# Transformer block: LN1 statistics of every second token tile on ScalarE, two min-adds of each q group on GpSimd, GpSimd's weight sums paced, two weight loads moved

## The chip, the cores and the metric

One core of one Trainium2 chip. The metric is device microseconds of one launch. The kernel before takes 759.02 us (median of 3 runs, 758.44 to 759.21). Engine names in the profile: PE is TensorE's matmuls, PEld its weight loads, DVE is VectorE, ACT is ScalarE, POOL is GpSimd ("Pool" below), SP is SyncE, which issues the DMAs. A bank is one of the buffers in PSUM in which TensorE adds up its products; a copy, sum or phi must have read it before TensorE can use it again.

## The reference

```python
# S=2048 tokens, D=1024, H=32 heads of 32, F=3584, inputs and weights bf16
phi = lambda t: where(t > 0, t + 1, exp(t)) + 1e-6
q, k, v = layernorm(x) @ wqkv          # split in three, by head
kv  = einsum("bhsd,bhse->bhde", phi(k), v)
z   = phi(k).sum over tokens
o   = (phi(q) @ kv) / (phi(q) . z + 1e-6)
h   = x + o @ wo
g   = layernorm(h)
h2  = h + (relu(g @ W_gate) * (g @ W_up)) @ W_down
```

(`gate * (gate > 0)` in the reference is the relu; the rest of its text sets up random inputs.)

## The kernel before

The kernel works in stages: the start and plain pieces for the first four token tiles; then, alternating, groups for k and v; q groups, in two halves of the tokens; the output projection; and the FFN in two passes of gate/up and down. The three projections use a scheme that forms a 2x2 block product from seven products (`P1` to `P7`) instead of eight, with sums of weights (`w_sums`, on Pool for q and v) and of tokens (`x_sums`, on VectorE) formed ahead.

One group, the same code for k, v and q. Seven products on TensorE; ScalarE copies (`ident_act`) fork one PSUM bank into another; what follows from a finished bank (`e11` to `e22`) is handed on in `pend` into the next group:

```python
def sgroup(pool, tok_major, X, SX, W, TW, e11, e12, e21, e22, name, hooks=()):
    # ... prod(): KH matmuls into one bank;  hook(i): pend[i] of the last group, then hooks[i]
    a = alloc_bank(pool); f = alloc_bank(pool); b = alloc_bank(pool)
    prod(a, X(0, 0), W(0, 0), True, "P1")
    ident_act(bank(b), bank(a), ..., name + "fk1")
    hook(1)
    prod(f, SX(2), TW(2), True, "P7")
    ident_act(s7, bank(f), ..., name + "s7")
    hook(2)
    c = alloc_bank(pool)
    prod(b, SX(1), TW(1), False, "P6")
    ident_act(bank(c), bank(b), ..., name + "fk2")
    hook(3)
    prod(a, X(1, 0), W(1, 0), False, "P2")
    # ... e11 on bank a
    hook(4)
    prod(c, SX(0), TW(0), False, "P5")
    ident_act(sc, bank(c), ..., name + "sc")
    # ... first step of e22
    hook(5)
    prod(b, X(1, 1), TW(3), False, "P4")
    # ... first step of e21
    hook(6)
    prod(c, SX(3), W(1, 1), False, "P3")
    pend[1] = list(e12(bank(c), B_bank[c]))
    pend[2] = list(s22[1:])
    pend[3] = list(s21[1:])
    hook(7)
```

phi is three operations: exp on ScalarE, then on VectorE a min-add, `min(e, 1) + 1e-6`, and `max(x + C1, that)`. The last one frees the PSUM bank or the SBUF buffer that it reads:

```python
def fin():
    PL.add("dve", lambda e: e.tensor_scalar(out=Et[:, k, :], in0=Et[:, k, :], scalar1=1.0,
                                            scalar2=1e-6, op0=ALU.min, op1=ALU.add), ...)   # "_e2"
    PL.add("dve", lambda e: e.scalar_tensor_tensor(out=dst_ap, in0=src, scalar=C1, in1=Et[:, k, :],
                                                   op0=ALU.add, op1=ALU.max), ...)          # "_phi"
```

LN1's statistics are on VectorE, the last step (variance to the power -0.5) on Pool, and each call of `ln1_stats` also issues a burst of Pool's weight sums behind it:

```python
def ln1_stats(st):
    i = st % NX1
    ln1_k[st] = ln_stats(x1[:, i, :], B_x1[i], "ln1_%d" % st)
    run(pool_q, {5: 8, 6: 5, 7: 4, 8: 5, 9: 5, 10: 5}.get(st, 7) if st >= 5 else 0)
```

In the output stage SyncE asks for transposes of `o`, for residual tiles, and, at some steps, for FFN weights; the down-projection weights (`load_wraw`) follow at its end:

```python
for t in range(NE, NST + LAG + 1):
    # ... a4 (output projection of tile t - LAG), a2 (num, division, transposes of tile t)
    if t in (5, 7, 9, 11, 18, 19):
        load_w_next()                 # 512 KB of gate or up weights
for q in range(NWR):
    load_wraw(q)
```

## Time and profile before

| TensorE's landmarks, from the trace | stage, us |
|---|---|
| start, to the first k piece | 7.79 |
| plain pieces and k group 2 | 32.14 + 20.55 |
| k and v groups 3 to 7 ("k/v stage" below) | 65.98 |
| q groups, first half / second half | 32.01 / 22.55 |
| output projection | 64.43 |
| FFN pass 0: gate/up, down | 169.43, 84.39 |
| FFN pass 1: gate/up, down and end | 169.21, 88.27 |

A stage ends at the first matmul of the next one, so a wait is counted in the stage that it delays. (The q halves and the output stage overlap by a few products at their landmarks. In this trace the record of the first matmul of FFN pass 0's down stage is missing: 0.22 us of the 169.43 belong to the 84.39.)

The head of the page, with the busy time of each engine in us (share of the span) and its number of instructions:

```profile
span 756.8 us, 10080 instructions
PE 737.7 (97%) x3547; PEld 337.2 (45%) x3603; DVE 545.6 (72%) x1083; ACT 291.2 (38%) x500; POOL 82.3 (11%) x148
```

TensorE is busy 737.7 of 756.8 us. (56 matmul records are missing from this trace, 3547 of 3603, so the true idle time is rather smaller than 19.1 us.) The list of TensorE's waits says on whom it waited (total us, times, longest):

```profile
PE ps L602 <- ACT ps L607: 3.9, 7, 1.2
PE ps L602 <- DMA RE<-RE: 2.3, 3, 1.2
PE ps L602 <- ACT RX L607: 1.9, 2, 0.9
```

`L607` is `ident_act`, so lines one and three are fork copies and copies to SBUF; the second is the transposes of `o` in the output stage. A q group of the second half in the timeline (start, length, engine, line, operation; in brackets the idle time before it and what ended it):

```profile
162.05 0.29 DVE L644 TENSOR_SCALAR RX<-RX 128x512 bf16<-128x512 bf16 x1
162.37 0.64 ACT L640 ACTIVATE RX<-RX 128x512 bf16<-128x512 f32 x1
162.38 0.69 DVE L647 SCALAR_TENSOR_TENSOR RAB<-ps,RX 128x512 bf16<-128x512 f32 x1
162.44 1.03 PE L602 MATMUL ps<-RAB,RO 128*128 128x512 bf16 x4
163.05 0.29 DVE L644 TENSOR_SCALAR RX<-RX 128x512 bf16<-128x512 bf16 x1
...
163.38 0.69 DVE L647 SCALAR_TENSOR_TENSOR RAB<-RX 128x512 bf16<-128x512 f32 x1
...
163.74 1.04 PE L602 MATMUL ps<-RWG,RH 128*128 128x512 f16 x4 [0.27 <-ACT ps L607]
```

exp (`L640`), min-add (`L644`, 0.29 us) and phi (`L647`, 0.69 us) follow each other, and TensorE loses 0.27 us in this stretch. The start (ScalarE's copies of the transposes, then the first k piece), and two of TensorE's longest waits in the k/v stage:

```profile
7.05 1.09 ACT L691 ACTIVATE RAB<-ps 128x512 bf16<-128x512 bf16 x2 [4.42 <-PE ps L688]
7.79 1.89 PE L602 MATMUL ps<-RAB 128*128 128x512 bf16 x8
...
80.58 1.04 PE L602 MATMUL ps<-RAB,RH 128*128 128x512 bf16 x4 [0.94 <-ACT RX L607]
...
84.58 1.04 PE L602 MATMUL ps<-RC,RWG 128*128 128x512 f16 x4 [1.23 <-ACT ps L607]
```

Two lines of the groups of work on Pool, which will matter later (busy us, mean ns of one):

```profile
L739 POOL TENSOR_TENSOR RW<-RAB 128x256 f16<-128x256 bf16 x16 | 13.4, 836 | 1.0
...
L1102 POOL TENSOR_TENSOR RO<-RWG 128x512 f16<-128x512 bf16 x4 | 4.6, 1153 | 0.0
```

### The profile page before, as it was taken

The page shows a single profiled execution, that of the slowest core. Times are in us where ns is not written, and L with a number is a line of the kernel's source. Part 1 is how long each engine was busy: PE and PEld are TensorE (multiplying, and loading weights), DVE is VectorE, ACT ScalarE, POOL GpSimd, SP SyncE. Part 2 cuts the span into 40 slices and gives each one's busy share as a digit, 9 for nine tenths or more (in the row PEclk, how much of TensorE's full clock was granted, in tenths as well). Part 3 has the DMA queues.
Part 4 walks back from the last instruction along what each step waited for, and adds up shares of the span by engine and source line. Part 5 has one row for each costly group of instructions (what it writes and reads, how often), then busy time and mean ns, then how long its engine had stood idle before and what let it go on. Part 6 is the DMA issues. An engine that isn't in the chain of part 4 may idle for free.

```text
span 756.8 us, 10080 instructions
## 1 busy us (share of the span) xinstructions
PE 737.7 (97%) x3547; PEld 337.2 (45%) x3603; DVE 545.6 (72%) x1083; ACT 291.2 (38%) x500; POOL 82.3 (11%) x148
## 2 busy tenths in 40 slices
PE   8999889999999999999999999999999999999998
PEld 3444334344544444444444444444444444444443
DVE  7978885889766798878877584847768686663343
ACT  4344545665850545454454100025454544520000
POOL 2746730000360000000000000000000000000000
PEclk9999999999999999999999999999999999999999
DMA  9753112402799786665445799743232231026664
GB/s 301 199 84 85 29 28 100 166 15 55 180 238 240 234 274 200 186 174 169 139 139 178 227 289 284 229 143 111 61 108 85 83 111 56 1 77 185 207 191 134
DMA packets 160225, 113.38 MB, mean 150 GB/s; under 512 B 51504, under 2 KB 141360, under 8 KB 160176
## 3 DMA queue, kind: packets, MB, share of 16 engines
q1 hardware_dynamic: 160176, 112.75, 52.3%
q8 instruction: 28, 0.46, 0.2%
q14 instruction: 21, 0.17, 0.1%
HBM read 85.46 MB, written 15.73 MB: 134 GB/s over the span
## 4 chain that ended last, share of the span: by engine, by line
PE 84%; DVE 8%; ACT 2%; issue 2%; SPq 1%; DMA 1%; POOL 0%; DVEq 0%; ACTq 0%; POOLq 0%
PE ps L602 84%; ACT ps L607 1%; DVE RX L644 1%; DVE RAB L647 1%; SPq L512 1%; DVE RE L647 1%; DVE RE L989 1%; DVE RWG L764 1%; ACT RX L640 1%; DVE RE L900 1%; DMA RE<-RE 1%; DVE st L615 1%; DVE RX L839 0%; SPq L508 0%; DVE RXH L629 0%
## 5 line engine op out<-in xcount | busy, mean ns | idle before, releaser
L607 ACT ACTIVATE ps<-ps 128x512 f32<-128x512 f32 x150 | 87.5, 583 | 199.5 <-PE ps L602 170.8
L602 PE MATMUL ps<-RC,RO 128*128 128x512 f16 x672 | 154.2, 379 | 0.0
L602 PE MATMUL ps<-RW,RAB 128*128 128x512 f16 (+1 forms) x681 | 150.1, 379 | 0.6
L602 PEld LDWEIGHTS ps<-RW,RAB 128*128 128x128 bf16 (+1 forms) x692 | 67.7, 98 | 81.6
L602 PE MATMUL ps<-RH,RWG 128*128 128x512 bf16 x435 | 103.0, 379 | 0.7
L602 PEld LDWEIGHTS ps<-RC,RO 128*128 128x128 f16 x672 | 65.7, 98 | 79.3
L607 ACT ACTIVATE RE<-ps 128x512 f32<-128x512 f32 x120 | 71.0, 597 | 76.1 <-PE ps L602 53.9
L602 PE MATMUL ps<-RC,RWG 128*128 128x512 f16 x296 | 71.1, 379 | 2.8 <-ACT ps L607 2.8
L602 PEld LDWEIGHTS ps<-RH,RWG 128*128 128x128 bf16 x448 | 43.8, 98 | 52.9
L1171 DVE TENSOR_TENSOR RAB<-ps,RAB 128x512 bf16<-128x512 f32 x28 | 19.3, 690 | 65.4 <-PE ps L602 65.4
L602 PE MATMUL ps<-RW,RE 128*128 128x512 bf16 x248 | 57.0, 379 | 2.8 <-DMA RE<-RE 2.3
L602 PE MATMUL ps<-RH,RO 128*128 128x512 bf16 (+1 forms) x242 | 58.3, 379 | 0.7
L602 PE MATMUL ps<-RAB 128*128 128x512 bf16 x239 | 56.6, 379 | 1.3 <-ACT RAB L691 0.7
L607 ACT ACTIVATE RAB<-ps 128x512 bf16<-128x512 f32 x56 | 33.4, 597 | 61.6 <-PE ps L602 61.6
L1102 DVE TENSOR_TENSOR RO<-RWG,RO 128x512 f16<-128x512 bf16 x108 | 45.3, 420 | 1.8
L602 PEld LDWEIGHTS ps<-RC,RWG 128*128 128x128 bf16 (+1 forms) x296 | 28.5, 98 | 38.9 <-ACT ps L607 5.4
L623 POOL TENSOR_TENSOR rstd<-ve,neghalf 128x1 f32<-128x1 f32 x24 | 14.4, 601 | 281.2 <-DVE ve L620 281.2
L1178 DVE TENSOR_TENSOR RE<-ps,RE 128x512 f32<-128x512 f32 x56 | 38.4, 690 | 5.0 <-ACT RE L607 5.0
L1102 DVE TENSOR_TENSOR RO<-RWG 128x512 f16<-128x512 bf16 x108 | 40.6, 417 | 0.0
L615 DVE BATCH_NORM_STATS2 st<-RE 128x6 f32<-128x512 bf16 x48 | 30.7, 680 | 12.8 <-DMA RE<-h_scr 11.9
L644 DVE TENSOR_SCALAR RX<-RX 128x512 bf16<-128x512 bf16 x64 | 23.1, 361 | 22.3 <-ACT RX L640 22.3
L1183 DVE TENSOR_TENSOR RE<-ps,RE 128x512 f32<-128x512 f32 x56 | 38.1, 681 | 0.0
(114 smaller groups left out, 792.0 us busy)
## 6 DMA issues: line engine op xcount, KB each, us to landing
RWG<-in_B_W_gate_dram SPq DMA_DIRECT2D x28, 512.0 KB, 3.7
RWG<-in_B_W_up_dram SPq DMA_DIRECT2D x28, 512.0 KB, 4.7
RW<-t_scr SPq DMA_DIRECT2D x56, 256.0 KB, 3.2
RW<-in_B_W_down_dram SPq DMA_DIRECT2D x42, 256.0 KB, 3.8
RW<-in_B_W_down_dram SPq DMA_DIRECT2D x14, 512.0 KB, 4.0
t_scr<-RW SPq DMA_DIRECT2D x14, 512.0 KB, 4.9
RE<-in_A_x_dram SPq DMA_DIRECT2D x23, 256.0 KB, 4.7
RAB<-in_A_wqkv_dram SPq DMA_DIRECT2D x8, 512.0 KB, 8.2
```

What stands on the lines that cost most here:

```text
L512: return PL.add("sp", lambda e: e.dma_start_transpose(dst_ap, src_ap), reads=reads, writes=writes, slot=slot, name=name)
L602: lambda e: e.matmul(out_ap, lhsT, rhs, start=start, stop=stop, skip_group_check=skip),
L607: PL.add("act", lambda e: e.activation(out=dst, in_=src, func=func), reads=reads, writes=writes, name=name)
L615: PL.add("dve", lambda e, c=c: e.bn_stats(out=st6[:, k, c * 6:(c + 1) * 6], in_=src_full[:, c * BCH:(c + 1) * BCH]), reads=[src_chunk_bufs ...
L623: PL.add("pool", lambda e: e.tensor_tensor(out=rstd[:, k, :], in0=ve[:, k, :], in1=neghalf[:], op=ALU.pow), reads=[B_ve[k], B_neghalf], wr ...
L640: PL.add("act", lambda e: e.activation(out=Et[:, k, :], in_=src, func=ACTF.Exp), reads=[src_buf], writes=[B_E[k]], name=name + "_exp")
L644: PL.add("dve", lambda e: e.tensor_scalar(out=Et[:, k, :], in0=Et[:, k, :], scalar1=1.0, scalar2=1e-6, op0=ALU.min, op1=ALU.add), reads=[] ...
L647: PL.add("dve", lambda e: e.scalar_tensor_tensor(out=dst_ap, in0=src, scalar=C1, in1=Et[:, k, :], op0=ALU.add, op1=ALU.max), reads=[src_bu ...
L1102: PL.add(eng, lambda e: e.tensor_tensor(out=Tring[:, k, j], in0=in0, in1=in1, op=ALU.subtract), reads=reads, writes=[B_T[k][j]], name="T%d ...
L1171: PL.add("dve", lambda e: e.tensor_tensor(out=hh[:, f1, 0:SBW], in0=bank(BA[1]), in1=r11[:, rr, :], op=ALU.mult), reads=[B_bank[BA[1]], B_ ...
L1178: PL.add("dve", lambda e, w=w: e.tensor_tensor(out=ftmp[:, 4 + w, :], in0=bank(BF_[w]), in1=ftmp[:, 2 + w, :], op=ALU.add), reads=[B_bank[ ...
L1183: PL.add("dve", lambda e, w=w: e.tensor_tensor(out=ftmp[:, 6 + w, :], in0=bank(BB[w]), in1=ftmp[:, w, :], op=ALU.add), reads=[B_bank[BB[w] ...
```

## The change

Its intent: take work off VectorE, which is the engine behind most of TensorE's waits, spread Pool's weight sums evenly so that they disturb VectorE less, and take load off SyncE's queue in the output stage. Six parts: (1) half of LN1's statistics in the k/v stage, and those of tile 1 in the start, become two passes on ScalarE; (2) Pool's sums are issued one by one from the hooks of the groups (each made to depend on the last ScalarE instruction issued so far); (3) two of the four min-adds of each q group go to Pool; (4) in q groups the fourth exp goes ahead of the next group's fork copy, and the division of `a2` goes behind a phi; (5) the start is reordered; (6) two weight loads leave the output stage. A small addition before the power moves from VectorE to Pool as well.

```diff
@@ statistics
+        def act_stats(src, src_bufs, junk, junk_buf, sv, svb, name):
+            def mean():
+                PL.add("act", lambda e: e.activation(out=junk, in_=src, func=ACTF.Identity, scale=1.0 / D,
+                                                     accum_out=sv[:, 0:1]), ...)
+            def square():
+                PL.add("act", lambda e: e.activation(out=junk, in_=src, func=ACTF.Square, scale=float(D) ** -0.5,
+                                                     accum_out=sv[:, 1:2]), ...)
+                # ... three small operations on Pool: mean^2 - EPS, difference, power
@@ phi
-        def phi_steps(src, src_buf, dst_ap, dst_buf, name):
+        def phi_steps(src, src_buf, dst_ap, dst_buf, name, eng="dve"):
...
-                PL.add("dve", lambda e: e.tensor_scalar(out=Et[:, k, :], in0=Et[:, k, :], scalar1=1.0,
-                                                        scalar2=1e-6, op0=ALU.min, op1=ALU.add),
+                PL.add(eng, lambda e: e.tensor_scalar(out=Et[:, k, :], in0=Et[:, k, :], scalar1=1.0,
+                                                      scalar2=1e-6, op0=ALU.min, op1=ALU.add),
@@ pacing
+        def pool_piece(n=1):
+            for _ in range(min(n, len(pool_q))):
+                pool_q.pop(0)(PL.prog["act"][-1])
@@ groups
-            pend[1] = list(e12(bank(c), B_bank[c]))
+            s12 = list(e12(bank(c), B_bank[c]))
+            if isq:
+                s12.pop(0)()
+            pend[1] = s12
@@ q_group
-                   add_phi(*dst(1, 0), "q_%d_%d" % (r, ct)),
-                   add_phi(*dst(1, 1), "q_%d_%d" % (r, ct)), "q%d%d" % (r, ct), hooks)
+                   add_phi(*dst(1, 0), "q_%d_%d" % (r, ct), "pool"),
+                   add_phi(*dst(1, 1), "q_%d_%d" % (r, ct), "pool"), "q%d%d" % (r, ct), hooks, True)
@@ start
         ln1_stats(0)
+        for f_ in ln1_stats_act(1):
+            f_()
         ln1_norm(0)
         # ... the loop over the first four tiles unrolled; T1(1..3) in the middle of a k piece
@@ k/v groups
-                if 2 * p + 4 < NST:
-                    ln1_stats(2 * p + 4)
+            def h_k5(p=p, sq=sq):
+                if 2 * p + 4 < NST:
+                    m_, q_ = ln1_stats_act(2 * p + 4)
+                    m_()
+                    sq.append(q_)
+                pool_piece()
+            # ... h_k6 issues q_; pool_piece() also in h_v1, h_v2, h_v5, h_v7 and
+            k_group(p, {1: pp, 2: pp, 3: h_k3, 4: pp, 5: h_k5, 6: h_k6, 7: pp})
@@ q groups, second half
-                    hooks[6] = lambda t=ct: a2(t)
+                    hooks[6] = lambda t=ct: a2_num(t)
                 q_group(r, ct, hooks)
+                if r == 1:
+                    pend[1].append(lambda t=ct: a2_div(t))
@@ output stage
-            if t in (5, 7, 9, 11, 18, 19):
+            if t in (5, 7, 18, 19):
                 load_w_next()
...
+        load_w_next()
+        load_w_next()
         for q in range(NWR):
             load_wraw(q)
```

(Cuts: renamed buffer counts, the same statistics helper used for LN2, bookkeeping.)

## The prediction

> **What bounds it now.** TensorE. The profile's first part gives PE 737.7 of 756.8 us busy, at granted clock 1.00. So all its idle time together is 19 us, 2.5%: no change off TensorE's own work can give much. The table of windows shows where it is idle: start (0 to 17 us) 2.7; k/v groups (60 to 121) 5.8; q groups (137 to 184) 1.5; output projection (184 to 236) 3.3; FFN (236 to 665) about 1; tail 4. The FFN and the tail, two thirds of the time, are hardly touched.
>
> **What the change does, by stage.**
>
> 1. *k/v groups.* The order of instructions shows TensorE's work unchanged. In the timeline the losses sit in v groups 4 and 5 (P3 waits 0.94 us for a ScalarE copy, the next k group's P6 1.23 us), both at the end of a VectorE chain: exp, phi, LN norm, two more phis, token sums, v add. While Pool's weight sums run that chain is inflated: min-add 0.28 to 0.76 us, phi from SBUF 0.69 to 1.11, norm 0.54 to 0.91. The Trainium skill ("SBUF — State Buffer", "Who interferes with whom") says VectorE and GpSimd share a port pair as an exclusive lock; the trace agrees: v groups 6 and 7, without Pool (and LN), take 6.4 us, groups 4 and 5 take 7.5; k groups 7.3 against 8.7. Pacing gives back part and spreads contention to groups 6, 7. VectorE loses 1.3 us of statistics in k groups 3 to 5, where it was often idle anyway; ScalarE gains two passes, about 1.24 us each (1.06 plus 0.19 reading the accumulator, seen in the output stage), just before fork copy fk1: I estimate 0.4 us of TensorE wait per such v group. Net gain 2 us (0 to 4.5).
>
> 2. *q groups.* P5 waits for fork copy fk2, late by 0.26 us in the first half and 0.43 in four groups of the second half, where VectorE is full. exp12 moves ahead of fk1 (0.5 us), the division behind a phi, two min-adds of 0.28 us per group go to Pool (estimate 0.6 us there). Gain 1.6 (0.8 to 2.2).
>
> 3. *Output stage.* SyncE issues without a break from 197 to 240 us, DMA share about 1.05; a4 waits for the o transposes 0.6+1.2+0.5 us. Two weight loads (1 MB) leave: gain 2.5 (1.2 to 3).
>
> 4. *FFN start.* Those loads now precede the down-projection weights that VectorE waited for (4.04 us, free for TensorE). These landed at 253.0; two more at 1.3 us each make it 2.6 us later, against an estimated slack of 2.6. Cost 0.3 (0 to 2).
>
> 5. *Start.* Tile 1's statistics on ScalarE in parallel, but the first rstd now needs two Pool operations (about 0.4 us more). About 0.
>
> **Sum:** 759.0 - 2 - 1.6 - 2.5 + 0.3, about 753.2 us; 8 in 10: 750 to 756.5. Faster by over 2%: 1% (needs 15 us, nearly all addressable idle time); within 2%: 97%; slower: 2%.
>
> **What would show it.** Right: v groups near 7 us and fewer 1 us waits at 75 to 105 us; q groups of the second half 6.6 to 6.8 us instead of 7.0; no a4 wait over 0.6 us on transposes; the first down-weight sums later than the FFN start by 10 us rather than 7.6, with TensorE not or little waiting. Wrong: new waits of P6 on fk1 behind the square pass; norm waiting for Pool; TensorE waits in FFN pairs 0 to 2.
>
> **What would make it wrong.** Pool pieces hitting VectorE's chain after all (gain 1 gone), ScalarE too full in k groups, weights of pair 1 or the down weights landing late, or losses simply moving to the next wait.

## The result and the profile after

The kernel after takes 778.77 us (median of 4 runs, 777.65 to 780.82), the kernel before beside it 758.82 us. The ratio is 1.0266, 95% interval 1.0242 to 1.029: slower by 2.7%. Ratios here are the mean time of one kernel's fast runs over that of the other's of the same rounds, so they are not quite the ratios of the medians quoted. The prediction was wrong, by 25.6 us and in its sign.

```profile
span 779.1 us, 10201 instructions
PE 747.8 (96%) x3603; PEld 337.6 (43%) x3603; DVE 531.8 (68%) x1028; ACT 302.4 (39%) x520; POOL 124.2 (16%) x185
```

VectorE has 14 us less to do, as intended. Pool has 42 us more, and in the chain of waits that ended last its share went from 0% to 3%. The stages say where the 22.3 us of span came from (the profiled execution is the slowest of the four; the medians differ by 20.0 us):

| stage, us | before | after | difference |
|---|---|---|---|
| start | 7.79 | 9.62 | +1.83 |
| plain pieces, k group 2 | 52.69 | 54.43 | +1.74 |
| k/v stage | 65.98 | 66.31 | +0.33 |
| q, first half | 32.01 | 38.72 | +6.71 |
| q, second half | 22.55 | 33.58 | +11.03 |
| output projection | 64.43 | 63.63 | -0.80 |
| FFN pass 0, gate/up | 169.43 | 170.69 | +1.26 |
| all the rest | 341.87 | 342.10 | +0.23 |

(0.22 us of the last row belong to the row above it, for the missing record told of above.)

TensorE's waits:

```profile
PE ps L604 <- DVE RAB L670: 10.7, 7, 1.8
PE ps L604 <- ACT RX L609: 6.4, 10, 1.0
...
PE ps L604 <- ACT RAB L731: 1.9, 1, 1.9
```

The first line is new: seven waits, up to 1.8 us each, on phi (`L670`) in the q groups. Why phi is late stands in the same list for VectorE, and in the groups of work on Pool:

```profile
DVE RAB L670 <- POOL RX L667: 28.1, 15, 3.3
```

```profile
L667 POOL TENSOR_SCALAR RX<-RX 128x512 bf16<-128x512 bf16 x16 | 34.3, 2142 | 53.8 <-ACT RX L663 53.2
```

VectorE stands idle for 28.1 us waiting for the min-add on Pool, one of which takes 2.14 us there. On VectorE it took 0.29. (2.14 is a mean: taken singly in the trace, nine of the sixteen take 1.92 to 1.95 us, and seven take 2.42 to 2.44. Each of these seven begins 0.04 to 0.05 us after a phi from SBUF on VectorE has begun; these phis take 0.69 us, no longer than others. So the two engines meet here too, but it is Pool that loses, 0.5 us at a time.) The same part of a q group as shown above, in the timeline of the kernel after:

```profile
166.89 4.42 POOL L667 TENSOR_SCALAR RX<-RX 128x512 bf16<-128x512 bf16 x2 [4.91 <-ACT RX L663]
...
168.84 0.69 DVE L670 SCALAR_TENSOR_TENSOR RAB<-RX 128x512 bf16<-128x512 f32 x1 [3.08 <-POOL RX L667]
...
169.56 0.60 ACT L609 ACTIVATE RX<-ps 128x512 f32<-128x512 f32 x1 [1.24 <-DVE RAB L670]
...
170.22 1.04 PE L604 MATMUL ps<-RH,RO 128*128 128x512 f16 x4 [0.50 <-ACT RX L609]
...
171.34 0.69 DVE L670 SCALAR_TENSOR_TENSOR RAB<-RX 128x512 bf16<-128x512 f32 x1 [1.81 <-POOL RX L667]
171.95 0.29 DVE L667 TENSOR_SCALAR RX<-RX 128x512 bf16<-128x512 bf16 x1
172.27 0.69 DVE L670 SCALAR_TENSOR_TENSOR RAB<-ps,RX 128x512 bf16<-128x512 f32 x1
...
173.02 1.04 PE L604 MATMUL ps<-RAB,RO 128*128 128x512 bf16 x4 [1.77 <-DVE RAB L670]
```

Read it from the top. Pool works off both min-adds of the group in 4.42 us. VectorE waits 3.08 us for the first; its phi then releases the SBUF buffer that ScalarE's copy at 169.56 overwrites, and that copy releases P3 (0.50 us lost). VectorE then waits 1.81 us for the second min-add; behind it in VectorE's order stand the min-add and phi of another bank, which wait for nothing of Pool's, but do not run before 171.95. That phi releases the PSUM bank of the next group's P1, at 173.02: 1.77 us lost. So a group of 7.0 us takes 9.3.

The start (same columns):

```profile
6.67 1.06 ACT L633 ACTIVATE RXH<-RE 128x1024 bf16<-128x1024 bf16 x1 [4.04 <-DMA RE<-in_A_x_dram]
...
7.85 1.06 ACT L638 ACTIVATE RXH<-RE 128x1024 bf16<-128x1024 bf16 x1
...
8.90 1.06 ACT L731 ACTIVATE RAB<-ps 128x512 bf16<-128x512 bf16 x2
...
9.62 1.02 PE L604 MATMUL ps<-RAB 128*128 128x512 bf16 x4 [1.90 <-ACT RAB L731]
...
12.12 3.37 PE L604 MATMUL ps<-RAB 128*128 128x512 bf16 x8
```

The two statistics passes over tile 1 (`L633`, `L638`) cannot begin before tile 1 has landed, at about 6.6 us, and stand in ScalarE's order ahead of the copies of tile 0's transposes (`L731`), which TensorE needs first: 1.90 us lost. The last line holds a second surprise: eight matmuls in 3.37 us, 427 ns from start to start, where 216 ns is usual in this trace. There are three such stretches of half rate in the trace after (12.1, 182.4 and 203.0 us); before has none between 5.4 and 756 us. The table of windows, cut in steps of 3.413 us (behind the window and its length come the busy us of PE, PEld, DVE, ACT and POOL with their counts, then the granted clock, the DMA share and GB/s):

```profile
8.41:11.82 3.41, 1.39 (x10) 0.69 (x11) 1.95 (x4) 1.56 (x4) 1.46 (x4) 0.98 1.07 378
11.82:15.24 3.42, 3.42 (x13) 1.46 (x12) 2.55 (x6) 1.68 (x3) 0.77 (x3) 0.52 1.10 357
...
179.07:182.48 3.41, 1.17 (x5) 0.44 (x6) 1.78 (x4) 1.02 (x2) 1.56 (x1) 0.98 0.08 14
182.48:185.89 3.41, 3.41 (x9) 1.18 (x8) 3.31 (x7) 0.58 (x1) 0.00 (x0) 0.52 0.00 0
...
189.31:192.72 3.41, 1.77 (x14) 0.76 (x11) 1.56 (x4) 1.19 (x2) 2.32 (x1) 1.00 0.00 0
...
199.55:202.96 3.41, 1.33 (x6) 0.43 (x7) 1.94 (x4) 0.86 (x2) 1.41 (x1) 0.98 0.03 6
202.96:206.37 3.41, 3.41 (x10) 1.23 (x9) 3.31 (x7) 1.23 (x2) 2.27 (x2) 0.52 0.01 2
```

The Trainium skill ("TensorE: Matmul & The Clock Gate", Part 1, "What's actually happening") tells of a free-running window of 3413 ns after which an idle TensorE is granted half its clock. The trace fits that. Its clock records, from which the column of the granted clock is formed, put the three stretches at 11.68, 182.35 and 202.83 us, each 3.41 us long, and these starts lie 50 and 6 times 3.413 us apart. (The windows above were cut 0.13 us too late, so they show 0.98 and 0.52; cut at the records' edges they read 1.00 and 0.50.) In the window before each stretch TensorE was busy for 1.25, 1.14 and 1.20 us of the 3.41. A window with 1.64 us, at 161.87, was not followed by one. On the grids of runs 1, 2 and 4 windows at full clock with 1.16 to 1.42 us were followed by half rate, but one of run 2 with 1.42 us was not, and those with 1.70 us and more were not. So the border lies near 1.4 us here, and it is not sharp to the accuracy of the modelled ends. One stretch costs at most eight matmuls of 427 instead of 216 ns, an estimate of 1.7 us. It depends on how the waits fall on the grid, and so differs from one execution to the next. Much of the spread among runs goes with the granted clock that the record lists for each: the two executions of run 2 at clock 1.00 took 778.1 and 778.5 us, the two at 0.995 and 0.996 took 781.5 and 780.4.

### The profile page after: what moved, and what is told of

It is laid out like the page before. It is cut to its first block, busy times and chain, and to the rows that moved or that the text cites. A ratio compares the mean times of both kernels' runs of the same rounds, so it can differ in the third digit from the quotient of the medians.

```text
span 779.1 us, 10201 instructions
## 1 busy us (share of the span) xinstructions
PE 747.8 (96%) x3603; PEld 337.6 (43%) x3603; DVE 531.8 (68%) x1028; ACT 302.4 (39%) x520; POOL 124.2 (16%) x185
## 4 chain that ended last, share of the span: by engine, by line
PE 83%; DVE 6%; ACT 3%; POOL 3%; issue 2%; DMA 2%; SPq 1%; DVEq 0%; ACTq 0%; POOLq 0%
PE ps L604 83%; POOL RX L667 2%; ACT RX L663 1%; DVE RAB L670 1%; DVE RWG L806 1%; DMA RE<-in_A_x_dram 1%; ACT ps L609 1%; ACT RX L609 1%; DVE RX L667 1%; DVE RE L670 1%; SPq L510 1%; DMA RE<-RE 1%; ACT RXH L633 0%; ACT RXH L638 0%; DVE RE L945 0%
## 5 line engine op out<-in xcount | busy, mean ns | idle before, releaser
L604 PE MATMUL ps<-RH,RWG 128*128 128x512 bf16 x448 | 106.0, 379 | 0.4 <-DVE RAB L1211 0.4
L604 PE MATMUL ps<-RH,RO 128*128 128x512 bf16 (+1 forms) x256 | 61.2, 380 | 4.5 <-ACT RX L609 4.5
L604 PE MATMUL ps<-RW,RE 128*128 128x512 bf16 x256 | 59.1, 387 | 2.5 <-DVE RAB L670 1.8
L604 PE MATMUL ps<-RAB 128*128 128x512 bf16 x248 | 59.6, 386 | 1.9 <-ACT RAB L731 1.9
L622 POOL TENSOR_SCALAR rstd<-mv 128x1 f32<-128x1 f32 x19 | 5.7, 299 | 265.6 <-DVE mv L620 265.6
L667 POOL TENSOR_SCALAR RX<-RX 128x512 bf16<-128x512 bf16 x16 | 34.3, 2142 | 53.8 <-ACT RX L663 53.2
L1218 DVE TENSOR_TENSOR RE<-ps,RE 128x512 f32<-128x512 f32 x56 | 38.3, 690 | 4.8 <-ACT RE L609 4.8
L604 PEld LDWEIGHTS ps<-RH,RO 128*128 128x128 f16 (+1 forms) x256 | 24.4, 98 | 35.5 <-ACT RX L609 7.1
L604 PEld LDWEIGHTS ps<-RW,RE 128*128 128x128 bf16 x256 | 24.7, 99 | 31.8 <-DVE RAB L670 2.3
```

What stands on the lines that cost most here:

```text
L604: lambda e: e.matmul(out_ap, lhsT, rhs, start=start, stop=stop, skip_group_check=skip),
L622: PL.add("pool", lambda e: e.tensor_scalar(out=rstd[:, k, :], in0=mv[:, k, 1:2], scalar1=EPS, scalar2=None, op0=ALU.add), reads=[B_mv[k]], ...
L667: PL.add(eng, lambda e: e.tensor_scalar(out=Et[:, k, :], in0=Et[:, k, :], scalar1=1.0, scalar2=1e-6, op0=ALU.min, op1=ALU.add), reads=[], ...
L1218: PL.add("dve", lambda e, w=w: e.tensor_tensor(out=ftmp[:, 4 + w, :], in0=bank(BF_[w]), in1=ftmp[:, 2 + w, :], op=ALU.add), reads=[B_bank[ ...
```

## The experiments

Thirteen kernels ran. All gave correct results but the third.

### 1. Only the two min-adds back on VectorE (a_qdve)

My theory: Pool's min-adds are the whole loss, and the rest of the change is worth some microseconds. Rivals: the new order of exp and division in the q groups is to blame, or Pool's and VectorE's contention for memory.

```diff
 # on the kernel after
-                   add_phi(*dst(1, 0), "q_%d_%d" % (r, ct), "pool"),
-                   add_phi(*dst(1, 1), "q_%d_%d" % (r, ct), "pool"), "q%d%d" % (r, ct), hooks, True)
+                   add_phi(*dst(1, 0), "q_%d_%d" % (r, ct)),
+                   add_phi(*dst(1, 1), "q_%d_%d" % (r, ct)), "q%d%d" % (r, ct), hooks, True)
```

> The changed kernel with the two min-adds of each q group back on VectorE, nothing else. Theory 1 (Pool's min-add, 2.14 us each in the trace of after where I had estimated 0.6, holds VectorE's phi and through it TensorE's banks; the half-rate matmuls near 182 and 203 us follow from the waits): the q groups lose their 17.7 us, the 427 ns matmuls behind them vanish (2.6 us), and the reordering gives about 1.5; time 755 to 759, granted clock 1.00. Theory 2 (the reordering of exp and division is what hurts, Pool's long operation only shows it): stays above 768.

Measured: 758.25 us (758.11 to 760.95), ratio 0.9998 (0.998 to 1.0015). The q halves took 31.34 and 21.69 us, less than before's 32.01 and 22.55. So two lines of the diff hold the 2.7%, and all the rest together is worth nothing. The half-rate stretches near 182 and 203 us are gone; the one of the start is left in the profiled execution (760.95 us, clock 0.998), while the other three, at clock 1.00, took 758.1 to 758.3. Against the third rival, the contention, speaks the length of VectorE's phis in the trace after: 0.69 us, whether a min-add ran on Pool at the time or not.

### 2. Only the two min-adds, on the kernel before (b_qpool)

```diff
 # on the kernel before
-                   add_phi(*dst(1, 0), "q_%d_%d" % (r, ct)),
-                   add_phi(*dst(1, 1), "q_%d_%d" % (r, ct)), "q%d%d" % (r, ct), hooks)
+                   add_phi(*dst(1, 0), "q_%d_%d" % (r, ct), "pool"),
+                   add_phi(*dst(1, 1), "q_%d_%d" % (r, ct), "pool"), "q%d%d" % (r, ct), hooks)
 # ... and phi_steps and add_phi with the argument eng, as in the change
```

> The kernel before with the two min-adds of each q group on Pool, nothing else. Theory 1: q groups of the first half 8.4 us and of the second about 9.3 us instead of 6.4 and 7.0, 15 to 21 us slower, 774 to 780. Theory 2: under 764. A third theory, that TensorE falls to half rate for a cause of its own and not because of the waits: no stretch of 427 ns matmuls after 20 us here; theory 1 expects such stretches where waits of about 1.8 us repeat.

Measured: 779.45 us (778.1 to 781.49), ratio 1.0271 (1.025 to 1.0291). The part alone gives the whole loss, from the other side: q halves of 41.22 and 33.92 us, Pool's min-add 2143 ns again. Its trace has half-rate stretches at 161.2 and 171.5 us, so the third theory falls. The waits alone cost most of it: at clock 1.00 two executions still took 778.1 and 778.5 us.

### 3. Other forms of the operation on Pool (a_forms)

Each of the eight q groups runs another form in the place of Pool's min-add, so that all are timed in one kernel. Its output is wrong (relative error 0.196). (A first draft with the minimum of two tensors on Pool did not build.)

```diff
 # on the kernel after; X_ = Et[:, k, :]; one form for each q group
+                forms = [
+                    lambda e: e.tensor_scalar(out=X_, in0=X_, scalar1=1.0, scalar2=1e-6, op0=ALU.min, op1=ALU.add),
+                    lambda e: e.tensor_scalar(out=X_, in0=X_, scalar1=1.0, scalar2=None, op0=ALU.min),
+                    lambda e: e.tensor_scalar(out=X_, in0=X_, scalar1=1e-6, scalar2=None, op0=ALU.add),
+                    lambda e: e.tensor_scalar(out=X_, in0=X_, scalar1=1.0, scalar2=1e-6, op0=ALU.mult, op1=ALU.add),
+                    lambda e: e.tensor_tensor(out=X_, in0=X_, in1=X_, op=ALU.mult),
+                    lambda e: e.tensor_tensor(out=X_, in0=X_, in1=X_, op=ALU.add),
+                    # ... the first form on 256 and on 128 columns only
+                ]
```

> The changed kernel, wrong on purpose: Pool's operation in the eight q groups takes eight forms, in order of the groups: min and add (as is), min alone, add alone, multiply and add (all tensor with scalars, 512 wide), tensor times tensor, tensor plus tensor (512 wide), min and add at 256 and at 128 wide. It measures why 2.14 us. If it is the two scalar operations in one: the single forms take 1.0 to 1.2 us and multiply-add 2.1. If it is min: min alone takes over 1.5 and multiply-add about 1.1. If any scalar form is slow on Pool: all three 512 wide scalar forms over 1.5 and the tensor-tensor forms near 1.15 as in the output stage. Widths 256 and 128 show the fixed part.

Measured, in the groups of work on Pool (`L669` to `L676` are the forms in the order above; the number behind the busy time is the mean in ns of one):

```profile
L669 POOL TENSOR_SCALAR RX<-RX 128x512 bf16<-128x512 bf16 x2 | 4.4, 2194 | 20.8 <-ACT RX L663 20.7
L671 POOL TENSOR_SCALAR RX<-RX 128x512 bf16<-128x512 bf16 x2 | 3.5, 1774 | 4.5 <-ACT RX L663 4.4
L670 POOL TENSOR_SCALAR RX<-RX 128x512 bf16<-128x512 bf16 x2 | 2.9, 1489 | 4.0 <-ACT RX L663 4.0
...
L673 POOL TENSOR_TENSOR RX<-RX 128x512 bf16<-128x512 bf16 x2 | 2.1, 1040 | 4.9 <-ACT RX L663 4.9
L672 POOL TENSOR_SCALAR RX<-RX 128x512 bf16<-128x512 bf16 x2 | 1.4, 710 | 5.3 <-ACT RX L663 5.3
```

Min and add together cost 2.19 us, min alone 1.49, add alone 1.77, and a multiply-add of the same shape 0.71. None of the three expected patterns came, and why min and add are slow and multiply-add is not stays open. The means mix two cases here as well: taken singly, min-add took 1.96 us and, begun just behind a phi from SBUF, 2.43; add 1.55 and 2.00; min 1.49 both times; multiply-add 0.62 and 0.80. On 256 columns min-add took 1.08 us and, behind a phi, 1.57, and on 128 columns 0.64: without a phi ahead, 0.64, 1.08 and 1.96 us for 128, 256 and 512 columns. The time goes with the width, so it is not a fixed price of the instruction. The lines of TensorE in this trace's timeline say what it means for the group: behind the min-adds of the first form TensorE lost 1.01 us at P3 and 0.91 us in the next group, behind those of `add` 0.60 and 1.34 us, and behind the multiply-adds, at 0.62 and 0.80 us each, nothing at all. In the second half, where VectorE has more to do, even the tensor-tensor forms at 1.04 us cost 0.47 us in each of their two groups. So a Pool operation of the 0.6 us that I had estimated would have fitted, in the first half at least. The kernel as a whole took 766.67 us (one run), between the two above, as a mix of forms should.

The Trainium skill ("GPSIMD Engine Reference", 3.1 "Elementwise — side-by-side cycle accounting") gives about 2.6 cycles for an element of a `tensor_tensor`, and for the best case of a loop 512 elements in 769 ns. With 1.2 GHz, as that section counts, its first figure makes an estimate of 1.11 us for 512 elements; 1.04 us was measured. The multiply-add at 0.71 us lies a little under the second figure. Nothing there would have told of 2.14 us for min-add.

### 4. The old start (a_start)

```diff
 # on the kernel after: the start of the kernel before
-        for f_ in ln1_stats_act(1):
-            f_()
         ln1_norm(0)
 # ... the unrolled part replaced by the loop over the first four tiles, with
+        ln1_stats(1)
```

> The changed kernel with the start as it was before (tile 1's statistics on VectorE, transposes and k pieces in the old order), the rest unchanged. If the start's loss (first k piece at 9.6 us instead of 7.8, then 8 matmuls at 427 ns) comes from ScalarE's two statistics passes standing ahead of the transposed tile's copies: 3 to 4 us faster than the changed kernel, 774.5 to 776, first k piece near 7.9 us, no 427 ns matmuls between 10 and 15 us. If it comes from the first rstd on Pool: the first k piece stays after 9 us.

Measured: 778.32 us (777.81 to 780.18), ratio 1.026, hardly less than after's 1.0266: the time that I expected, 774.5 to 776, was missed. In the profile (776.4 against 779.1 us of span) the start did what I expected: start and plain pieces to k group 2's first products took 40.13 instead of 43.51 us, as before. But in the same trace the second half of the q groups took 35.40 instead of 33.58 us, with two half-rate stretches (170 and 190 us) instead of one: a part of the gain was given back where the waits fell on the clock's windows in another way. With the waits gone (run 8 below against run 1) the start's worth shows: ratios 0.9974 against 0.9998, some 1.8 us. The two intervals overlap a little, and by the medians it is 0.6 us, so the size is not firm.

### 5 to 7. The moved loads, the q order, and both, on the kernel before (b_loads, b_qord, b_best)

```diff
 # b_loads, on the kernel before
-            if t in (5, 7, 9, 11, 18, 19):
+            if t in (5, 7, 18, 19):
...
+        load_w_next()
+        load_w_next()
         for q in range(NWR):
 # b_qord, on the kernel before: only the parts of the change with
+            if isq:
+                s12.pop(0)()
...
+                if r == 1:
+                    pend[1].append(lambda t=ct: a2_div(t))
 # b_best: both
```

> The kernel before with only the two weight loads moved behind the output stage. My prediction: output stage 2.5 us shorter, FFN start 0.3 longer, 756.6 to 757.5. Rival from the run with the min-adds back on VectorE: output stage 0.9 shorter, FFN pairs 0 and 1 1.3 us longer, so 758.5 to 760, no gain: what the transposes win, VectorE's later down-weight sums give back.

> The kernel before with only the order of the q groups changed (exp12 ahead of the fork copy, the division behind a phi), min-adds on VectorE. Expect q groups 1.2 to 1.8 us shorter together, 757 to 758; if the division's move only shifts the wait, no change (758.5 to 759.5).

> The two parts together (moved loads, q order) on the kernel before. If they add: 0.5 to 4 us under before, by the two runs above; if the loads give nothing, the same as the q order alone, 757 to 758.

Measured:

| kernel | us | ratio (95%) | stages that moved |
|---|---|---|---|
| b_loads | 757.48 | 0.9979 (0.9966 to 0.9991) | output 62.21 (64.43), FFN 169.79 (169.43), plain pieces +1.0 (a late weight tile in this execution) |
| b_qord | 757.23 | 0.9982 (0.9968 to 0.9995) | q 31.45 and 21.47 (32.01 and 22.55) |
| b_best | 756.08 | 0.9963 (0.995 to 0.9975) | output 62.51, q 31.45 and 21.47, FFN 169.92 |

Both parts are worth what the prediction said of them (output -2.2 for -2.5, q -1.6 for -1.6, and FFN +0.6 for +0.3, with the 169.43 of before put right to 169.21), and they add: 0.9979 times 0.9982 is 0.9961.

### 8. The kernel after with both bad parts undone (a_qdve_start)

```diff
 # on the kernel after: the edits of runs 1 and 4 together
```

> The changed kernel with the min-adds on VectorE and the start of before: what is left are ScalarE statistics and paced sums in the k/v groups, the q order and the moved loads. Theory: start's loss and Pool's min-adds are all of the slowdown, so 754 to 756.5, first k piece at 7.9 us, k/v groups as in the changed kernel (66.3 us). If the start costs nothing once nothing else waits: 758.

Measured: 757.42 us, ratio 0.9974 (0.9962 to 0.9987). That is more than the 754 to 756.5 that I expected. Beside b_best of the same rounds (756.08) it has, in addition, paced sums and statistics on ScalarE. It is not faster. Its k/v stage took 66.32 us, before's 65.98. So the predicted 2 us of the k/v stage are not there. The next runs ask why.

### 9. Bursts of Pool's sums as before, with the statistics on ScalarE (kv_burst)

```diff
 # on a_qdve_start: every pool_piece() out, and bursts where the kernel before has them
+        def burst(st):
+            run(pool_q, {5: 8, 6: 5, 7: 4, 8: 5, 9: 5, 10: 5}.get(st, 7) if st >= 5 else 0)
...
+                if 2 * p + 4 < NST:
+                    burst(2 * p + 4)
```

> As the changed kernel with VectorE min-adds and the old start, ScalarE statistics kept, but Pool's weight sums in bursts as before. It tells pacing from statistics in the k/v groups (66.0 us before, 66.3 changed, from first P7 of v group 3 to the first q group). If pacing is worth something: k/v groups over 67 us. If spreading the sums into groups 6 and 7 costs what it saves: 65 to 66.3, groups 6 and 7 back at 6.4 us, the waits of 1 us in v groups 4 and 5 again.

Measured: 763.25 us (761.75 to 764.62), ratio 1.006 (1.0045 to 1.0075); k/v stage 72.90 us. In its timeline, v group 4:

```profile
77.64 4.41 POOL L784 TENSOR_TENSOR RH<-RO 128x256 f16<-128x256 bf16 x6
...
82.70 0.56 POOL L647 TENSOR_TENSOR s<-s,neghalf 128x1 f32<-128x1 f32 x1
83.29 0.55 DVE L716 TENSOR_SCALAR RXH<-RE,s 128x1024 bf16<-128x1024 bf16 x1 [4.11 <-POOL s L647]
...
85.45 1.89 PE L604 MATMUL ps<-RAB,RH 128*128 128x512 bf16 x4 [4.35 <-ACT RX L609]
```

The norm waits 4.11 us for three tiny operations on Pool (`s`, the last of which takes 0.56 us), because these stand in Pool's order behind six weight sums of 0.7 us. TensorE loses 4.35 us, and then runs 12 matmuls at half rate (the clock records show 0.50 from 83.72 to 90.54 us, two windows on end; in the first of these TensorE was busy for 1.68 us, at half rate). So statistics on ScalarE make pacing necessary: their result comes late, and must then pass through Pool's queue.

### 10. Pacing alone (kv_dve)

```diff
 # on a_qdve_start: statistics of the even tiles on VectorE again
             def h_k3(p=p):
...
+                if 2 * p + 4 < NST:
+                    ln1_stats(2 * p + 4)
             def h_k5(p=p, sq=sq):
-                if 2 * p + 4 < NST:
-                    m_, q_ = ln1_stats_act(2 * p + 4)
-                    m_()
-                    sq.append(q_)
                 pool_piece()
```

> The same base, pacing kept, but the even tiles' statistics back on VectorE in the k groups. If ScalarE's two passes delay the fork copy of the next v group (0.1 us of wait at P6 there, and the exps behind it): k/v groups 0.3 to 1.5 us shorter than 66.3. If VectorE needed the relief: longer by 1 us or more. If neither matters: within 0.2.

Measured: 755.2 us (754.75 to 756.32), ratio 0.9953 (0.9936 to 0.9969), k/v stage 64.64 us. Pacing by itself gains 1.34 us of this stage (65.98 to 64.64), and the statistics on ScalarE cost 1.68 (64.64 to 66.32): each of v groups 3 to 5 takes 7.23 us with them and 6.39 without, and each k group behind them 0.28 us less. (kv_dve also has the small addition on Pool, which before has on VectorE; it was not tested alone.) The prediction's "2 us" was two effects of opposite sign.

### 11. Pool's sums in k groups and plain pieces only (kv_konly)

If what remains is contention in the v groups, where VectorE's chain is the longest, the sums should leave them. In kv_dve the v groups take 6.39 us and the k groups 8.35: I read this as work of VectorE that is late in a v group and delays the k group behind it. (The expectation has the v groups drop; at 6.39 us they had done so already.)

```diff
 # on kv_dve: no pool_piece() in h_v1, h_v2, h_v5, h_v7; in the plain pieces two at a time, and
-            k_group(p, {1: pp, 2: pp, 3: h_k3, 4: pp, 5: h_k5, 6: h_k6, 7: pp})
+            k_group(p, {1: pp, 2: pp2, 3: h_k3, 4: pp2, 5: k5, 6: k6})      # pp2: two pieces
```

> The last one with Pool's sums issued in the k groups and the plain pieces before them alone, none from v groups. If VectorE's chain in the v groups (phi and norm from SBUF) is held by Pool, v groups 3 to 7 drop to 6.4 to 6.9 us without the waits of 0.8 and 1 us, k/v groups 62.5 to 64.5 us, the kernel 2 to 3 us faster than the paced one. If the chain is that long without Pool: no change.

Measured: 754.34 us (752.95 to 755.64), ratio 0.9943 (0.9928 to 0.9958). That is 0.9 us less than kv_dve, not 2 to 3. The k/v stage took 61.38 us, with k groups of 7.6 us, but the stage ahead of it lost 1.9 us: TensorE waited 1.80 us at 55.4 us. In the timeline a norm there had waited 1.40 us for the power operation on Pool, with the token sums behind it in VectorE's order; Pool was then under two sums for each plain piece.

### 12 and 13. One sum at a time in the plain pieces (kv_best2), and the down weights first (kv_best3)

Two questions were open here: whether that 1.80 us wait was Pool's queue, and whether the loss at the start of the FFN (0.6 to 2.0 us in all kernels that move the loads) is the order of SyncE's requests.

```diff
 # kv_best2, on kv_konly
-        pool_piece(6)
+        pool_piece(8)
...
-        pool_piece(4)
+        pool_piece(6)
...
-                pool_piece(2)
+                pool_piece()
...
-            k_group(p, {1: pp, 2: pp2, 3: h_k3, 4: pp2, 5: k5, 6: k6})
+            k_group(p, {1: pp2, 2: pp2, 3: h_k3, 4: pp2, 5: k5, 6: k6})
 # kv_best3, on kv_best2
-        load_w_next()
-        load_w_next()
         for q in range(NWR):
             load_wraw(q)
+        load_w_next()
+        load_w_next()
```

> The kernel before with all that earlier runs found good (two weight loads moved, division and exp order in the q groups, statistics on VectorE, Pool's weight sums paced one by one in k groups and plain pieces only), and the sums of the plain pieces one at each piece instead of two, with more of them earlier. If the 1.8 us wait of TensorE at 53 to 55 us of the run with two per piece came from the norm's rstd standing behind nine queued Pool sums, it is gone or below 0.6 us, the stage from the first v piece group to the q groups is at most 61.4 us, the stage before it at most 21 us, and the time is 0.4 to 2 us under that run's, 752.4 to 754 us, ratio about 0.992. Rival: the wait is VectorE's own chain (token sums behind the copies), then it stays at 1.4 us or more and the time stays at 754 to 755.

> The run above with one change: at the end of the output stage the down-projection weights are asked for ahead of the two moved weight loads, as in the kernel before, and the two loads follow them. If the FFN start loss (0.4 to 1.3 us in all runs that move the loads) is the down weights landing 2.6 to 3.4 us later behind the two loads, then their landing is again about 8 us after the FFN start, the first FFN stage takes 169.2 to 169.5 us instead of 170.0 to 170.8, and the time is 0.4 to 1.2 us under the run above. Rival: the moved loads themselves are needed early (FFN pairs 1 to 2), then new TensorE waits on a weight DMA appear in the first 60 us of FFN and the time is the same or longer.

Measured: kv_best2 752.28 us (752.03 to 752.43), ratio 0.9909 (0.9894 to 0.9924); kv_best3 749.59 us (749.28 to 749.61), ratio 0.9874 (0.9858 to 0.9891); both beside 759.32 us of the kernel before. In kv_best2 the 1.80 us wait is gone and the k/v stage takes 60.75 us, 5.2 less than before. Its start of the FFN:

```profile
250.95 1.04 PE L604 MATMUL ps<-RH,RWG 128*128 128x512 bf16 x4 [1.09 <-DVE RAB L1211]
```

VectorE, which forms sums of the down weights, waited for them until 248.7 us, and TensorE in turn for VectorE. The down weights landed at 248.66 us in this kernel, 11.9 us after the start of the FFN, behind the two moved loads; in kv_best3 at 244.63 us, 8.4 us after it. There the first FFN stage takes 169.21 us instead of 171.42, and the list of TensorE's waits in kv_best3 holds no wait of the FFN any more, neither on sums nor on the moved weights:

```profile
PE ps L604 <- POOL RXH L475: 1.4, 1, 1.4
PE ps L728 <- DVE RXH L652: 0.9, 1, 0.9
PE ps L604 <- DVE RE L1038: 0.7, 1, 0.7
```

The gain of kv_best3 over kv_best2, 2.7 us, is larger than the 0.4 to 1.2 us that I expected: in the profiles 2.2 us are the FFN's, and 0.45 us the start's (first k piece at 7.84 instead of 8.29 us), which the edit does not touch. kv_best3 is 1.3% faster than the kernel before, the best of all that ran; its span is 747.6 us with TensorE busy for 739.0.

## Why the prediction was wrong

- **The step that failed: "two min-adds of 0.28 us per group go to Pool (estimate 0.6 us there)", within "Gain 1.6 (0.8 to 2.2)" for the q groups.** The prediction named no source for the 0.6 us. The min-add took 2.14 us there, three and a half times the estimate. It sits in a chain (exp, min-add, phi) whose last link frees a buffer and a bank that TensorE needs, and VectorE stood still for it, 28.1 us in all. Instead of gaining 1.6 us the q groups lost 17.7 (runs 1 and 2: the two lines alone are +2.7% on either kernel). The mechanism that I named as the danger, "Pool pieces hitting VectorE's chain", was right in kind, but I had it in the k/v stage only. Run 3 shows that the size decides: with an operation of 0.71 us on Pool TensorE lost nothing in its group, the last of the first half.
- The estimate could have been better with what the profile of before held: Pool took 0.84 us for a 256 wide sum, and 1.15 us for a 512 wide one. No arithmetic in that profile was as fast as 0.6 us at this width (only a memset was, 0.52 us). Even so, 2.14 us was not to be read from it; it depends on the two operations chosen, as run 3 shows.
- **"Start. About 0": wrong.** Start and plain pieces lost 3.6 us in the profile, by two statistics passes standing ahead of the copies that TensorE needs first. Undone, they come back in the profile (run 4); in time they are worth about 1.8 us (runs 1 and 8).
- **"k/v groups. Net gain 2 us": wrong, 0.3 us lost.** Pacing gained 1.34 us as meant, the ScalarE passes cost 1.68: 0.84 us for each of three v groups, twice the 0.4 that I had set against it, less 0.28 in each k group behind (run 10). The contention fits what was measured: the Trainium skill ("SBUF — State Buffer", "Who interferes with whom") says that VectorE and Pool share one port pair under an exclusive lock, and with Pool's sums in the k groups alone, these fell from 8.35 to 7.4 us beside v groups of 6.39 us as they were, and the stage took 60.75 us instead of 65.98 (runs 10 to 12). That was worth more than the prediction thought, by another edit than the change's. How much of it is the port and how much Pool's queue ahead of LN's small operations (run 9) is not separated.
- **The rest of "q groups", right:** the order of exp and division gained 1.6 us of the stages (run 6).
- **"Output stage. Gain 2.5" and "FFN start. Cost 0.3", right** in run 5 (2.2 and 0.6). In the changed kernel itself the output stage gained 0.8 us only, and the FFN's start lost 1.5. That loss follows one number, the time from the FFN's first matmul to the landing of the first down weights: at 7.6 to 8.4 us (before, runs 2, 6 and 13) nothing is lost; at 10.3 us (run 5) 0.6, at 10.6 (run 11) 0.9, at 11.2 (after) 1.5, at 11.7 (run 10) 2.0, at 11.9 (run 12) 2.2. So the slack ends near 9.7 us, and putting the down weights first took the loss away.
- **Not foreseen at all: half-rate stretches.** Three in the profiled execution, at most 1.7 us each by the estimate above, so up to 5 of its 22.3 us. The waits alone come to more: run 2 at clock 1.00 was still 19 us slower. I had counted waits at their own length only.
- "Faster by over 2%: 1%" was right in its reason: nearly all idle time would have to go. The 2% for slower was far too low for a change that puts a new engine with an estimated duration into TensorE's chain in every q group.

Left open: whether Pool could take the min-adds if phi were issued a group later, so that VectorE did not wait; why min and add take so long on Pool; and how much of the spread among runs is the clock's, as only one execution of each kernel has a trace.

## What to carry to other kernels

Before work moves to another engine, find the same operation in the same form there in a trace, or time it alone, and ask who waits for its end: 2 us on an engine that is 84% idle cost 20 us because an in-order engine stood behind it. Where an engine takes both bulk work and tiny operations that a chain waits for, issue the bulk work piece by piece where nothing of the chain is in its queue. When a change of many parts comes out even or worse, split it: here three of its parts (pacing and the moved loads, both rearranged, and the q order), together with the small addition on Pool, make a kernel 1.3% faster than the one before.

## What the Trainium skill lacked or had wrong

- "GPSIMD Engine Reference", 3.1: figures for `tensor_tensor` and for the best case of a loop only. Lacking: a `tensor_scalar` of min and add on 128x512 bf16 takes 2.14 to 2.19 us in the mean (1.92 to 1.96 undisturbed, 2.42 to 2.44 when begun just behind a phi from SBUF on VectorE), min alone 1.49, add alone 1.77, multiply and add 0.71.
- "TensorE: Matmul & The Clock Gate", Part 1: it names an idle window of some 3.4 us as the cause of half rate, and "HAM oscillation" there warns of idle gaps of over 3.4 us. "A second HAM failure mode" there says that frequent short idle times can do it too, but gives no threshold. Here waits of 0.5 and 1.8 us with work between them sufficed: at full clock, windows of 3.41 us in which TensorE was busy for 1.14 to 1.42 us were followed by half rate (after, runs 1, 2 and 4), one with 1.42 us was not (run 2), and those with 1.64 us and more were not. The durations agree: 427 ns from start to start at half rate, 216 ns at full.
- No page that I found has a price for statistics on ScalarE with an accumulator: a pass over 128x1024 bf16 took 1.06 us, and reading the accumulator 0.19 us more.
